# Token transform of a fused attention and Fourier kernel: even and odd tokens apart, on four 32-row parts of the TensorE array

## The chip, the cores and the metric

The kernel runs on one core of a Trainium2 chip. The metric is the device time of one execution in microseconds (us). A core has the engines that the profile calls PE (TensorE, matmuls), DVE (VectorE), ACT (ScalarE), POOL (GpSimd) and SP (SyncE, which here only issues DMAs). Each engine works through its own queue in order; they wait for each other by semaphores.

## The reference, cut to what matters

All in float32. Chunked attention gives `x`; then a Fourier mix over tokens and channels, of which the real part is added; then a normalised two-layer MLP.

```python
q, k, v: (8 batches, 8 heads, 576 tokens, 64)      # chunks of 64 tokens
attn = softmax(q_c @ k_c.T / 8);  x = attn @ v_c    # -> x: (8, 576, 512)
mixed = real(fft(fft(x, axis=tokens), axis=channels))
u = x + mixed
un = (u - mean) / sqrt(var + 1e-6)                  # over channels
out = u + relu(un @ w_ch1) @ w_ch2                  # 512 -> 2048 -> 512
```

The change is about the first of the two transforms: over the 576 tokens, for each of 8 batches. A real input needs cosine and sine sums at frequencies 0 to 288 only; the others follow by mirroring.

## The kernel before, in words

**Tiles.** 128 tokens by 512 channels. A batch of 9 chunks has two LO tiles (chunks 0 to 3), two HI tiles (chunks 8 to 5, held mirrored) and half of a REST tile (chunk 4), which it shares with its neighbour. A *group* is four tiles that go through the MLP together: 8 groups of LO and HI tiles, one per batch, and a last one of the four REST tiles.

**Order.** It is written out by hand. The main loop at the end of the kernel steps through `mlp(g)`, group after group. After each step it lets a *side* generator run on by a share that is counted out so that the side is done when group `g + 1` is due: `side(b)` is `attention(b)`, a pause of three steps, then `fourier(b)`. What a generator does between two `yield`s is put into the engines' queues between two steps of the MLP. In groups 2 to 8 a step is mostly eight matmuls of 128x128 by 128x256. The weights are converted during the first group (`round_weight`), and combined and kept in DRAM (`keep1`, `keep2`) so that the later groups need seven half-size products in place of eight; SP fetches these in slabs (`fetch`).

**From attention to transform.** A token n and its mirror 576 - n share cosine and sine up to sign, so `fold(b, i)` adds and subtracts LO and HI tile and does the same over channels: `pm` has four parts T of 128 channels, and one column more for channel 256. For tokens to stand opposite their mirrors, the first row of each LO chunk has to move on by one chunk: `shift(b)` does this for five rows (L485 to L489), from batch 2 on with six DMAs in SP's queue, through a small tile `first`.

**`fourier(b)`, b from 1 to 7.** For each T it multiplies 128 tokens x 128 channels with the token table `tk` (128 x 289 frequencies), over two full tiles and then the 64 rows of REST: 12 matmuls at L652, and 12 with a single column for channel 256. T = 0, 1 come between one pair of steps, T = 2, 3, REST and the single columns between the next pair. ACT takes the four results out of PSUM into `zf` and `zr` (L678 to L688); then comes the channel transform, three or two times `mixed(i)` (L700), and DVE and POOL add it to x. Batch 0 has its own form, `fourier_early`, before the main loop. In `attention_early`, `turn_tables` (L252 to L254, ACT) reorders the loaded table into `tk`.

**`store(n, o)`** writes a finished tile: one DMA for LO, two for HI, all from SP; four for REST, half of them from ACT in the last group.

Of the kernel before, what the change touches and what calls it, by code (L numbers as in the profile page):

```python
# [8 lines left out]
FP32 = mybir.dt.float32  # L9
# [7 lines left out]
def kernel(  # L17
# [67 lines left out]
    tk = const.tile([128, NM + 1, 2, NQ], FP32, name="tk")  # L85
# [3 lines left out]
    so = const.tile([128, HQ], FP32, name="so")  # L89
    wa = const.tile([128, KD * DFF], FP32, name="wa")  # L90
# [71 lines left out]
    pms, sts = {}, {}  # L162
    start = one_p.tile([128, KF * 512], FP32, tag="big", name="start")
# [5 lines left out]
    v_ring = [const.tile([128, 2, NJ, DV], FP32, name=f"v{i}") for i in range(3)]  # L169
    more_v = one_p.tile([128, 4 * NL + 64], FP32, tag="zf", name="more_v")  # L170
# [4 lines left out]
    def load(n, which="qk"):  # L175
# [4 lines left out]
        for src, dst, nm, eng in ((q, qs, "q", nc.sync), (k, ks, "k", nc.scalar if n == 0 else nc.sync)):  # L180
            if nm not in which:
                continue
            if n < first[1]:
                i = 2 * n + (nm == "k")
                t = start[:, (4 + i) * DM:(5 + i) * DM].rearrange("p (j r d) -> p j (r d)", r=2, d=D)
            else:
                t = one_p.tile([128, NJ, 4 * D], FP32, tag=nm, name=nm)
# [36 lines left out]
    def load_tables():  # L224
# [4 lines left out]
        t = start[:, 0:(NM + 1) * 2 * NQ].rearrange("p (i r f) -> p i r f", i=NM + 1, r=2)  # L229
        for c in range(2 * NM):  # L230
            (i, r0), (j, p0) = divmod(c * CH, 128), divmod((NC - 1 - c) * CH, 128)
            nc.sync.dma_start(out=t[r0:r0 + CH, i], in_=seq_tab[p0:p0 + CH, j])
        for r0 in (0, CH):
            nc.sync.dma_start(out=t[r0:r0 + 1, NM], in_=seq_tab[0:1, 0])
            nc.sync.dma_start(out=t[r0 + 1:r0 + CH, NM], in_=seq_tab[1:CH, NM])
# [11 lines left out]

    def turn_tables():
        t = start[:, 0:(NM + 1) * 2 * NQ]
        a, b = tk.rearrange("p i r f -> p (i r) f"), t.rearrange("p (i f) -> p i f", f=NQ)  # L250
        for c in range(2 * NM):
            nc.scalar.copy(a[:, :, c * CH:(c + 1) * CH], b[:, :, (c + 1) * CH:c * CH:-1])  # L252
        nc.scalar.copy(a[:, :, NL:NL + 1], b[:, :, 0:1])
        nc.scalar.copy(a[:, :, NL + 1:NQ], b[:, :, NL + 1:NQ])  # L254
# [157 lines left out]
    def att_P(n):  # L412
# [3 lines left out]
        nc.scalar.copy(t, pt)  # L416
# [46 lines left out]

    def shift_early(i):

        lows = [xt(at[LO, 0, j])[:, 0:DM] for j in range(NM)]
        rest, kept = xt(rests[0])[0:1, 0:DM], first_rest[0:1, 0:DM]
        if i == 0:
            nc.gpsimd.tensor_copy(kept, lows[1][0:1])
            nc.gpsimd.tensor_copy(lows[1][0:1], lows[1][CH:CH + 1])  # L470
            nc.gpsimd.tensor_copy(lows[1][CH:CH + 1], rest)
        else:
            nc.scalar.copy(rest, lows[0][0:1])
            nc.scalar.copy(lows[0][0:1], lows[0][CH:CH + 1])
            nc.scalar.copy(lows[0][CH:CH + 1], kept)

    def shift(b):

        lows = [xt(at[LO, b, i]) for i in range(NM)]
        r = b % 2 * CH  # L480
        rest = xt(rests[b // 2])[r:r + 1, 0:DM]
        eng = nc.gpsimd if b < 2 else nc.sync
        t = three_p.tile([128, XW], FP32, tag="y", name="first")
        for i in range(NM):
            eng.dma_start(out=t[2 * i:2 * i + 2, 0:DM], in_=lows[i][0:CH + 1:CH, 0:DM])  # L485
        eng.dma_start(out=t[2 * NM:2 * NM + 1, 0:DM], in_=rest)
        for i in range(NM):
            eng.dma_start(out=lows[i][0:CH + 1:CH, 0:DM], in_=t[2 * i + 1:2 * i + 3, 0:DM])
        eng.dma_start(out=rest, in_=t[0:1, 0:DM])  # L489

    def fold(b, i):
# [7 lines left out]
        if i < NM:  # L499
            pm = two_p.tile([128, DM + 1], FP32, tag="pm", name="pm")  # L500
# [5 lines left out]
        else:  # L506
            pm = two_p.tile([128, 2 * HQ + 1], FP32, tag="pm_rest", name="pm_rest")
# [10 lines left out]
        if i < NM:  # L518
# [3 lines left out]
            to = pm[:, 3 * HQ:DM + 1:HQ]  # L522
        else:
            for T, op in enumerate((ALU.add, ALU.subtract, ALU.subtract, ALU.add)):
                to = pm[T % 2 * CH:T % 2 * CH + CH, T // 2 * HQ:T // 2 * HQ + HQ]
                eng.tensor_tensor(out=to, in0=near[:, T // 2], in1=far[:, T // 2], op=op)
            to = pm[CH:, HQ:2 * HQ + 1:HQ]
        eng.tensor_copy(to, two[p, HM + 1 + HQ:HQ - 1:-HM - 1])
        pms[b, i] = pm

    def attention_early():
# [33 lines left out]
        turn_tables()  # L565
# [64 lines left out]
    zr = const.tile([128, 4, 2, CH], FP32, name="zr")  # L630
# [12 lines left out]

    def fourier(b):
        h = b % 2
        zf = one_p.tile([128, 4 * NL + 64], FP32, tag="zf", name="zf")
        zf = zf[:, 0:4 * NL].rearrange("p (t f) -> p t f", t=4)
        pm = [pms.pop((b, i)) for i in range(NM + 1)]

        def product(T, i, out_, lhsT, start, stop, cols=slice(0, NQ)):  # L650
            p = slice(0, 128) if i < NM else slice(T % 2 * CH, T % 2 * CH + CH)
            nc.tensor.matmul(  # L652
                out=out_, lhsT=lhsT[p], rhs=tk[p, i, T // 2 if T != 5 else 0, cols],
                start=start, stop=stop, skip_group_check=True,
            )


        z = [ps_t.tile([128, 512], FP32, tag="pt", name="z") for _ in range(2)]
        more = ps_a.tile([128, 2, 512], FP32, tag="att", name="more_z")
        z += [more[:, k] for k in range(2)]  # L660
        for T in range(4):
            for i in range(NM):
                product(T, i, z[T][:, 0:NQ], pm[i][:, T * HQ:(T + 1) * HQ], i == 0, False)
            if T == 1:
                yield
        for T in range(4):
# [629 lines left out]
```

## Time and profile before

| what | value |
|---|---|
| runs | 1093.8, 1089.85, 1092.42 us; median 1092.42 |
| profiled execution | span 1089.0 us; no time of its own is listed apart from the three runs, of which the lowest is 0.85 us and the median 3.4 us above the span |
| busy share of the span | PE 98%, DVE 53%, ACT 27%, POOL 26% |
| granted TensorE clock | full speed in all 40 slices |
| chain that ended last | PE 89%, DVE 4%, ACT 2%, DMA 2%, SP's queue 2% |
| L652, token transform | PE share of the chain 1.5% (`z`) and 1.7% (`more_z`) |
| end of the last matmul's record | about 1084.2 us, then DVE, the last DMAs, the end |

In the trace one float32 matmul of the code stands as two MATMULs, each with a LDWEIGHTS; counts below are those of the trace unless "of the code" is said. A line of the timeline gives the start, the time from the first start to the last end, the engine, the line of code, what is written and read, the shape and how many. Because matmuls are pipelined, the step from one start to the next, not the duration, is what one costs.

### The profile page before, as it was taken

The page shows a single profiled execution, that of the slowest core. Times are in us where ns is not written, and L with a number is a line of the kernel's source. Part 1 is how long each engine was busy: PE and PEld are TensorE (multiplying, and loading weights), DVE is VectorE, ACT ScalarE, POOL GpSimd, SP SyncE. Part 2 cuts the span into 40 slices and gives each one's busy share as a digit, 9 for nine tenths or more (in the row PEclk, how much of TensorE's full clock was granted, in tenths as well). Part 3 has the DMA queues.
Part 4 walks back from the last instruction along what each step waited for, and adds up shares of the span by engine and source line. Part 5 has one row for each costly group of instructions (what it writes and reads, how often), then busy time and mean ns, then how long its engine had stood idle before and what let it go on. Part 6 is the DMA issues. An engine that isn't in the chain of part 4 may idle for free.

```text
span 1089.0 us, 18837 instructions
## 1 busy us (share of the span) xinstructions
PE 1070.4 (98%) x7018; PEld 848.7 (78%) x7018; DVE 577.2 (53%) x1258; ACT 299.2 (27%) x730; POOL 280.3 (26%) x403
## 2 busy tenths in 40 slices
PE   8999999999999999999999999999999999999998
PEld 6644454446888888888888888888888888888887
DVE  4899987314566355663556455735663534323411
ACT  4788453222113310322022212321133103101300
POOL 4301002444405140153114220514051401210140
PEclk9999999999999999999999999999999999999999
DMA  7777556679575637692668357854653455446232
GB/s 167 224 222 175 158 162 227 171 239 308 178 203 167 198 136 206 189 255 95 191 184 253 124 165 223 206 170 152 197 185 90 147 190 163 120 154 211 78 116 78
DMA packets 147970, 192.73 MB, mean 177 GB/s; under 512 B 66126, under 2 KB 104014, under 8 KB 140712
## 3 DMA queue, kind: packets, MB, share of 16 engines
q1 hardware_dynamic: 145620, 190.20, 58.4%
q8 instruction: 56, 0.92, 0.4%
q0 software_dynamic: 512, 0.68, 0.3%
q10 hardware_dynamic: 1748, 0.66, 0.2%
q14 instruction: 34, 0.28, 0.1%
HBM read 167.22 MB, written 24.12 MB: 176 GB/s over the span
## 4 chain that ended last, share of the span: by engine, by line
PE 89%; DVE 4%; ACT 2%; DMA 2%; SPq 2%; issue 1%; POOL 0%; DVEq 0%; ACTq 0%
PE pb L1089 20%; PE pa L1040 17%; PE pa L1089 15%; PE pb L1040 13%; PE up L973 4%; PE up L953 3%; PE pt L333 3%; PE dn L994 3%; PE mix L700 2%; PE sc L384 2%; PE more_z L652 2%; PE xp L432 2%; PE z L652 1%; PE idle L1167 1%; DMA xall<-in_moe_w_ch_dram 1%; SPq L195 1%
## 5 line engine op out<-in xcount | busy, mean ns | idle before, releaser
L1040 PE MATMUL pa<-unT,wa 128*128 128x256 f32 x672 | 159.5, 380 | 1.1 <-DVE wa L1048 1.1
L1040 PEld LDWEIGHTS pa<-unT,wa 128*128 128x128 f32 x672 | 126.5, 190 | 18.9 <-DVE wa L1048 1.5
L941 POOL TENSOR_TENSOR h<-h 128x256 f32<-128x256 f32 x64 | 55.7, 877 | 269.5 <-PE pb L1040 150.5
L1089 PE MATMUL pa<-wb,h 128*128 128x256 f32 x512 | 115.6, 380 | 0.0
L1089 PE MATMUL pb<-wb,h 128*128 128x256 f32 x512 | 114.9, 379 | 0.0
L1040 PE MATMUL pb<-wa 128*128 128x256 f32 x448 | 106.6, 381 | 0.0
L1089 PEld LDWEIGHTS pa<-wb,h 128*128 128x128 f32 x512 | 96.1, 190 | 13.5 <-issue 0.5
L1089 PEld LDWEIGHTS pb<-wb,h 128*128 128x128 f32 x512 | 96.3, 190 | 12.6
L1040 PEld LDWEIGHTS pb<-wa 128*128 128x128 f32 x448 | 84.2, 190 | 11.6 <-DVE h L1056 0.2
L994 PE MATMUL dn<-wb,h 128*128 128x512 f32 x128 | 58.4, 605 | 0.9 <-ACT h L964 0.9
L1046 DVE TENSOR_TENSOR wa<-pb,wa 128x256 f32<-128x256 f32 x56 | 23.5, 423 | 65.5 <-ACT wa L1045 65.5
L1089 PE MATMUL pb<-wb,yall 128*128 128x256 f32 x256 | 58.2, 381 | 0.0
L1089 PE MATMUL pa<-wb,yall 128*128 128x256 f32 x256 | 57.9, 380 | 0.0
L1089 PE MATMUL pb<-wb 128*128 128x256 f32 x256 | 57.7, 379 | 0.0
L973 PE MATMUL up<-unT,wa 128*128 128x512 f32 x128 | 56.8, 596 | 0.0
L1045 ACT COPY wa<-pa 128x256 f32<-128x256 f32 x56 | 20.8, 372 | 125.1 <-PE pa L1040 125.1
L1040 PE MATMUL pa<-wa 128*128 128x256 f32 x224 | 53.5, 382 | 0.0
L717 POOL TENSOR_TENSOR xall<-y,xall 128x513 f32<-128x513 f32 x14 | 21.3, 1518 | 125.3 <-DVE y L711 125.3
L1040 PE MATMUL pb<-unT,wa 128*128 128x256 f32 x224 | 52.9, 379 | 0.0
L1089 PEld LDWEIGHTS pa<-wb,yall 128*128 128x128 f32 x256 | 47.7, 190 | 6.4
L1089 PEld LDWEIGHTS pb<-wb,yall 128*128 128x128 f32 x256 | 47.7, 190 | 6.3
L1089 PEld LDWEIGHTS pb<-wb 128*128 128x128 f32 x256 | 47.6, 190 | 5.9
(250 smaller groups left out, 1685.0 us busy)
## 6 DMA issues: line engine op xcount, KB each, us to landing
wb<-s SPq DMA_DIRECT2D x56, 1024.0 KB
wa<-s SPq DMA_DIRECT2D x196, 256.0 KB
xall<-in_moe_w_ch_dram SPq DMA_DIRECT2D x22, 512.0 KB
q<-in_q_dram SPq DMA_DIRECT2D x96, 112.0 KB
k<-in_k_dram SPq DMA_DIRECT2D x96, 112.0 KB
v<-in_v_dram SPq DMA_DIRECT2D x124, 64.0 KB
yall<-in_moe_w_ch_dram SPq DMA_DIRECT2D x10, 512.0 KB
s<-wb SPq DMA_DIRECT2D x20, 256.0 KB
```

Source lines behind the costliest of these rows:

```text
L333: nc.tensor.transpose(pt[:, j, :], src(j), ident)
L384: nc.tensor.matmul(out=sc[t0:t0 + CH, e, j * CH:(j + 1) * CH], lhsT=a[r0:r0 + D, 2 * j + c, 0:CH], rhs=b[r0:r0 + D, 2 * j + c, 0:CH], star ...
L432: nc.tensor.matmul(out=xp[0][e][t0:t0 + CH, j * DV:(j + 1) * DV], lhsT=a[r0:r0 + CH, j, t0:t0 + CH], rhs=b[r0:r0 + CH, c, j, :], start=Tru ...
L652: nc.tensor.matmul(out=out_, lhsT=lhsT[p], rhs=tk[p, i, T // 2 if T != 5 else 0, cols], start=start, stop=stop, skip_group_check=True,)
L700: nc.tensor.matmul(out=mix[:, cols], lhsT=zt[:, T], rhs=tab, start=(T == 0), stop=(T == 3), skip_group_check=True,)
L941: nc.gpsimd.tensor_tensor(out=h1[:, m, hi], in0=h1[:, m, lo], in1=h1[:, m, hi], op=ALU.subtract)
L953: nc.tensor.matmul(out=up, lhsT=w1[:, kk, m * 128:(m + 1) * 128], rhs=unT[:, kk], start=(kk == 0), stop=(kk == KD - 1), skip_group_check=True,
L973: nc.tensor.matmul(out=up, lhsT=w1[:, kk, m * 128:(m + 1) * 128], rhs=unT[:, kk], start=(kk == 0), stop=(kk == KD - 1),)
L994: nc.tensor.matmul(out=dn, lhsT=h1[:, m, s * 128:(s + 1) * 128], rhs=w2[:, m, :], start=(m == 0), stop=(m == KF - 1),)
L1040: nc.tensor.matmul(out=dst, lhsT=w[:, kk, r], rhs=rhs[o][:, kk], start=(o in (0, 1) and kk == 0), stop=(kk == 1), skip_group_check=True,)
L1046: nc.vector.tensor_tensor(out=b, in0=pbs[r][:, 0], in1=a, op=ALU.add)
L1089: nc.tensor.matmul(out=dst, lhsT=lhs[:, m], rhs=w[:, m], start=(o in (0, 2) and m == 0), stop=(m == HF - 1), skip_group_check=True,)
```

## The change

It rewrites the token transform of batches 1 to 7, and reorders the tokens of each chunk for it.

- Tokens of a 64-token chunk are held with 32 of one parity first, then 32 of the other. `att_P` does this while it copies the transposed probabilities out of PSUM (same ACT copy, other access pattern). `store` and the table loads follow the order.
- The table `tk` shrinks to frequencies 0 to 144 (NE = 145). For frequency f and 288 - f the sums over even tokens are equal up to sign, and so are those over odd tokens; so even and odd sums are formed apart, and then E + O and E - O give both halves.
- `z_sets` computes these with matmuls of 32 rows: four of the code in a row, one for each 32-row part, each to another PSUM bank. 40 such matmuls of 32x128 by 32x145 per batch, in two sets ("turns") of 24 and 16, take the place of 12 of 128 or 64 rows by 289.
- `mid_products`: the single column for channel 256, now two columns (as it is, and with the sign of the parity, made by one more small operation in `fold`); 12 matmuls of one column as before.
- ACT copies the odd sums (`z_odd`), DVE forms sum and difference (`z_joined`), ACT then spreads the result into `zf` and `zr` (`z_tile`, `z_rest`). There is one more `yield`, and `sizes` counts one more.
- The table is loaded once, in full length, to a part of `wb`; `fourier_early` uses it from there, and ACT copies the half that is kept to `tk` after step 8. `turn_tables` is gone.
- `shift` for b > 1 is six GpSimd copies of one row each, in place of six DMAs of SP.
- `store`: two DMAs for LO, four for HI of which ACT issues two, five for REST.
- Three unused tiles are allocated as padding, and some tiles are declared elsewhere.

```diff
-    tk = const.tile([128, NM + 1, 2, NQ], FP32, name="tk")
+    NE = NQ // 2 + 1
+    tk = const.tile([128, NM + 1, 2, NE], FP32, name="tk")
...
+    const.tile([128, 48], FP32, name="pad_a")
...
-        nc.scalar.copy(t, pt)
+        nc.scalar.copy(
+            t.rearrange("p j (c r i) -> p (j c) r i", c=2, r=2), pt.rearrange("p j (c i r) -> p (j c) r i", c=2, r=2)[:, :, ::-1]
+        )
...
-        eng = nc.gpsimd if b < 2 else nc.sync
+        eng = nc.gpsimd
         t = three_p.tile([128, XW], FP32, tag="y", name="first")
+        if b > 1:
+            kept, r0, r1 = t[0:1, 0:DM], slice(ODD, ODD + 1), slice(ODD + CH, ODD + CH + 1)
+            a, c = lows[0][:, 0:DM], lows[1][:, 0:DM]
+            for to, from_ in ((kept, rest), (rest, a[r0]), (a[r0], a[r1]), (a[r1], c[r0]), (c[r0], c[r1]), (c[r1], kept)):
+                eng.tensor_copy(to, from_)
+            return
...
         eng.tensor_copy(to, two[p, HM + 1 + HQ:HQ - 1:-HM - 1])
+        eng.tensor_tensor(out=pm[rows, m0 + 1:m0 + 2], in0=pm[rows, m0:m0 + 1], in1=sign[rows], op=ALU.mult)
...
-        turn_tables()
...
+    def z_sets(z, pm, i, turn_, first=False):
+        for s in range(2):
+            for q_ in range(4):
+                k, r = (q_ // 2 + turn_) % 2, q_ % 2
+                T, p = 2 * k + s, slice(32 * q_, 32 * q_ + 32)
+                d0_ = T * HQ if i < NM else s * HQ
+                nc.tensor.matmul(
+                    out=z[r][k][:, s * NE:(s + 1) * NE], lhsT=pm[i][p, d0_:d0_ + HQ],
+                    rhs=tk[p, NM - 1 - i if i < NM else NM, k],
+                    start=first and s == 0, stop=False, skip_group_check=True,
+                )
...
+    def z_odd():
+        for k in range(2):
+            nc.scalar.copy(zs[0][:, 2 * k:2 * k + 2, 1], zs[2][k][:, 0:2 * NE].rearrange("p (t f) -> p t f", t=2))
+
+    def z_joined():
+        even = zs[1][:, :, 0:2 * NE].rearrange("p k (t f) -> p k t f", t=2)
+        z4 = zs[0].rearrange("p (k t) r f -> p k t r f", t=2)
+        nc.vector.tensor_tensor(out=z4[:, :, :, 0], in0=even, in1=z4[:, :, :, 1], op=ALU.add)
+        for k in range(2):
+            e, o = even[:, k], z4[:, k, :, 1]
+            a, b = (e, o) if k == 0 else (o, e)
+            nc.vector.tensor_tensor(out=o, in0=a, in1=b, op=ALU.subtract)
...
+        z = z_space()
         for i in range(NM + 1):
+            z_sets(z, pm, i, 0, i == 0)
+        outs = [z[0][0][32 * g:32 * g + 1, 2 * NE:] for g in range(4)]
+        for i in range(NM):
+            mid_products(outs, pm, i)
+        nc.scalar.copy(middle[:, 0, 0:1], outs[0][:, 0:1])
+        yield b == 1
+        if b == 1:
+            yield
+        mid_products(outs, pm, NM)
+        for i in range(NM):
+            z_sets(z, pm, i, 1)
+        z_middle(outs)
+        z_odd()
+        if b == 1:
+            z_joined()
+        else:
+            yield
+            z_joined()
+        nc.scalar.copy(zs[0][0:1, 2], middle)
+        if h == 1:
+            z_rest(h)
+        for i in range(NM):
+            z_tile(zf, i)
+        if h == 0:
+            z_rest(h)
+        yield b == 1
...
+            elif kind(n) == RE:
+                eng = nc.scalar if last and h else nc.sync
...
             else:
-                nc.sync.dma_start(out=out[b, t0:t0 + CH, :], in_=o[r0:r0 + CH])
+                for r in range(2):
+                    eng = nc.scalar if r else nc.sync
+                    eng.dma_start(out=out[b, t0 + 1 - r:t0 + CH:2, :], in_=o[r0 + ODD * r:r0 + ODD * r + ODD])
+        if kind(n) == RE:
+            eng.dma_start(out=out[b - 1:b + 1, 0, :], in_=o[LONE])
...
+                if t == 8:
+                    nc.scalar.copy(tk, early_tk[:, :, :, 0:NE])
```

`z_tile` makes five ACT copies of at most 256 elements per partition, `z_rest` five smaller ones, `z_middle` four of one row.

## The prediction

> **What bounds the kernel now.** I read the busy table first, then the chain that ended last, then the timeline of PE around one `fourier(b)`.
>
> ```profile
> PE 1070.4 (98%) x7018; PEld 848.7 (78%) x7018; DVE 577.2 (53%) x1258; ACT 299.2 (27%) x730; POOL 280.3 (26%) x403
> ...
> PE 89%; DVE 4%; ACT 2%; DMA 2%; SPq 2%; issue 1%; POOL 0%; DVEq 0%; ACTq 0%
> ```
>
> PE is busy throughout and is 89% of the chain, the others have half their time free. So what leaves PE's queue is nearly a gain of the same size, and what is added elsewhere costs only if PE must wait for it. The block of batch 7 (the last column before a bracket is the count):
>
> ```profile
> 827.90 2.11 PE L652 MATMUL z<-tk,pm 128*128 128x289 f32 x8
> 829.85 1.89 PE L1040 MATMUL pa<-unT,wa 128*128 128x256 f32 x8
> 831.58 2.11 PE L652 MATMUL more_z<-tk,pm 128*128 128x289 f32 x8
> 833.62 0.76 PE L652 MATMUL z<-tk,pm_rest 64*128 64x289 f32 x4
> 834.21 0.66 PE L652 MATMUL more_z<-tk,pm_rest 64*128 64x289 f32 x4
> 834.79 0.43 PE L652 MATMUL more_z<-tk,pm 128*1 128x73 f32 x16
> 835.16 0.30 PE L652 MATMUL more_z<-tk,pm_rest 64*1 64x73 f32 x8
> 835.39 0.48 PE L1089 MATMUL pa<-wb,h 128*128 128x256 f32 x1
> ```
>
> From start to start: 8 full MATMULs of 289 columns take 829.85 - 827.90 = 1.95, or 0.244 each. Four with 64 rows take 0.59, where one after the other would be 0.98: two run at a time. Sixteen with one output column take 0.37; at 0.244 x 73 / 289 = 0.062 each that would be 0.99: they run four at a time. The rest of each stretch, 0.10 to 0.12, is the change from one form to the next. The first MATMUL after it has 0.48 in place of 0.38: its weights were not loaded ahead (0.10). The block costs 1.95 + (835.39 - 831.58) + 0.10 = **5.86**, seven blocks 41.
>
> **What the Trainium skill says.** "TensorEngine Tiling (Array Packing)", Key Properties: parts of the array load weights and multiply in parallel, and a change of the tiling mode drains the engine. The trace agrees: two or four at a time, 0.10 to 0.12 for a change. Same page, Restrictions and Gotchas: row parts that run together must write to different PSUM banks. In the changed code the bank is z[q_%2][(q_//2+turn)%2], four banks for four parts; before, `z` and `more_z` did so for two parts. "TensorE: Matmul & The Clock Gate", Part 3: four parts of 32 rows gave 3.07x, not 4x (512 columns). No run here shows four row parts; the nearest row is `sc`, four quarters of 64x64 at a time:
>
> ```profile
> 283.18 0.69 PE L384 MATMUL sc<-kT,qT 64*64 64x64 f32 x32
> 283.80 0.91 PE L1089 MATMUL pb<-wb,h 128*128 128x256 f32 x3
> ```
>
> 32 in 0.62; 8 slots of 64 columns are 8 x 0.054 = 0.43, and 0.19 is getting in and out. So four at a time cost little more than one.
>
> **The change, part by part.**
>
> *Token products.* 40 matmuls of the code, 80 MATMULs of 145 columns. One needs 0.244 x 145 / 289 = 0.122; loading 128 weight columns needs no more than 0.113 (two 128x128 `mix` products start 0.225 apart). I take 0.125 a slot: 80 / 4 x 0.125 = 2.50. The single columns stay 24 MATMULs, 6 slots of 0.062 = 0.37. Changes of form: in, to columns, out, in both halves, 6 x 0.12 = 0.72, and a weight load not hidden (0.10) at two entries and two exits, 0.40. Sum 3.99, gain 5.86 - 3.99 = 1.87, **seven times -13.1**. With the skill's 3.07 in place of 4 the slots are 3.26 and the gain is 7.8.
>
> *Evacuation.* ACT has 18 operations a block as before, of about the same sizes, and DVE three new ones, about 0.7 + 0.42 + 0.42 = 1.5 (estimate from L710, 255 elements in 0.42). The chain from the last token product to `mix` is longer: `z_odd`, DVE 1.5, the copy of the middle row 0.4, `z_rest` about 1.0 (odd b). From batch 2 on two MLP steps (2 x 3.45) stand between the join and `mix`, and the join of odd batches first waits for two DVE adds (0.84) at the end of the up half: 3.7 of 6.9. Cost nothing; if that cover is gone, what exceeds 6.9, per block. One more wait: the last single columns wait for a one-element ACT copy issued a step earlier; hidden likewise. The even banks are held a stage longer, but no `turn` or score matmul falls into that stage.
>
> *Batch 1* has one step as cover, and today it stalls:
>
> ```profile
> 152.06 0.49 PE L700 MATMUL mix<-ce,zr 128*128 128x129 f32 x2 [1.12 <-ACT zr L681]
> 152.51 0.49 PE L700 MATMUL mix<-co,zr 128*128 128x128 f32 x2
> 153.82 1.22 PE L700 MATMUL mix<-cx,zr 128*128 128x256 f32 x2 [0.82 <-ACT zr L688]
> 154.83 0.63 PE L700 MATMUL mix<-so,zr 128*128 128x128 f32 x2
> ```
>
> These four took 3.2 to the next `dn`, against 1.1 in batch 7, after 1.1 of waiting: 3.2 lost, because ACT stood behind weight conversion. In the change two of the three gaps put no conversion ahead, but the chain is 0.8 + 0.8 + 1.5 + 0.4 + 1.0 = 4.5 against a step of 3.4. So 1 to 2 are lost in place of 3.2. I take **-1.0** (from -2.2 to +1.5).
>
> *`shift`.* In SP's queue its six DMAs of batch 4 stand from 455.38 to 459.6, ahead of weight slabs and the next q and k. The chain shows what that led to:
>
> ```profile
> 456.05 1.78 DMA first<-xall
> ...
> 462.14 4.16 DMA q<-in_q_dram
> ...
> 467.84 1.99 PE pa L1040 x8
> ```
>
> PE lost 1.2 ahead of 467.84; the other batches' DMAs delayed nothing that shows. Gone: **-1.2** (0 to -1.5). On POOL six copies at 0.60 (L469, 1x512) are 3.6 a batch, six batches. Behind them wait `fold` and the subtraction L941, which the down half needs only in its fourth product, over 20 us later; POOL is 74% idle. Nothing. The sign column adds three operations of 0.2 per `fold`: POOL for b > 1, DVE for b = 1, hidden by the pause of three steps.
>
> *Start.* Without `turn_tables` the first token product need not wait for ACT until 31.77; the warm-up matmuls end at 31.45: -0.3. `zr` takes 15 ACT operations in place of 10, at a spacing of 0.09, before L641, which had 0.21 of slack: +0.25. SP issues ten table DMAs in place of eight, so the channel tables come up to 0.6 later; POOL is done with them at 37.6 and PE wants them at about 38.9: covered. The copy of `tk`, 870 elements by the rate of L252 (384 in 0.44) 1.0, is among ACT's ReLUs, between 0 and +1.0; I take **+0.3** for the whole start.
>
> *`store`.* SP: six `shift` DMAs less, two LO stores more per batch. ACT now issues two DMAs for each of 16 HI tiles behind a DVE result, and, as built, behind an earlier DMA of SP's queue. Behind them in ACT's queue is `pT`, which PE needs a step (3.45) later: 0.42 + 0.65 + 0.58 = 1.65, so 1.8 of slack, which a late SP can use up. Not shown in the trace; between 0 and +4, I take **+1.0**. At the end ACT issues three DMAs in place of two: **+0.3** (L883, 0.26 to 0.36).
>
> *Padding* moves addresses only; nothing in the trace prices it. PE's MATMULs already start 0.216 apart for 256 columns, so 0, from -1 to +1.
>
> Sum: -13.1 - 1.0 - 1.2 + 0.3 + 1.0 + 0.3 = **-13.7** on the span of 1089.0: 1075.3. The median of the runs is 3.4 above that span; I keep this: 1078.7.
>
> **Rivals.**
>
> *A. Four row parts run at 3.07.* For it: the skill's figure. Against: `sc` at four a time. 5.3 less gain: 1084.
>
> *B. Only two at a time, slower.* The two passes of a matmul sit on the same part, so a queue kept strictly in order would overlap neighbours only. Against: the 0.59 for four REST MATMULs includes the first weight load, so passes are interleaved, and `sc`. Place: L676; price: 40 slots, +2.5 a block, 17.5 in all: 1096. The gain of all parts is gone below 2.2 at a time (slots of 4.46 per block).
>
> *C. ACT's queue becomes the wait.* HI stores hold ACT for SP, `pT` or `unT` comes late, PE idles 0.5 to 1 at each of 16 tiles: 1086 to 1094. For: two queues now in series. Against: SP has fewer DMAs.
>
> *D. `mix` waits in every block,* 1 to 2 each, if DVE is behind: 1086 to 1093. Against: DVE 53% busy, about 3 of slack.
>
> *E. The queue was not the cause:* q and k come late in batch 4 all the same: +1.2, inside the range.
>
> **How the numbers follow.** Forecast as summed 0.58, A 0.20, C 0.08, B 0.08, D 0.06. About 0.3% (3.3 us) is what a measurement of this kernel can tell from no change. Faster than 1089: the forecast, A, and part of C and D, 0.83. Same: rest of C and D, 0.06. Slower: B, and C or D at their worst or together, 0.11. Range: below, all unknowns at their good end, about 1071; above, past A to where C begins, 1089.
>
> **What would show it.** Right: the 24 and 16 row-part matmuls take 1.7 and 1.2 (0.125 a slot), L676 and L686 together about 4.0 a block; no `first` DMA in SP; no idle of PE before `mix` beyond 1 from batch 2 on. Wrong: 0.16 a slot or more (A), 0.25 (B), PE released by ACT `pT` next to a store (C), `mix` released by ACT `zf` or `zr` (D).

## The result: 3.65% slower

After the change the kernel takes 1129.07 us (median of 4 runs, 1127.49 to 1136.71) against 1091.96 before in the same comparison: ratio 1.0365, 95% interval 1.0338 to 1.0392. The profiled execution took 1130.52 us, its span is 1128.7. The prediction was 1078.7 and "faster": wrong, by 50 us. The token products, which bring the gain, behaved as predicted; five things around them, each costed at next to nothing or not at all, and some smaller ones lost more than three times what was gained.

The page of the kernel after, busy table and chain that ended last:

```profile
PE 1069.4 (95%) x7410; PEld 847.0 (75%) x7410; DVE 586.3 (52%) x1287; ACT 308.6 (27%) x730; POOL 306.6 (27%) x459
...
PE 74%; DMA 4%; issue 2%; SPq 1%; DVE 1%; POOL 1%; ACT 1%; DVEq 0%; POOLq 0%; ACTq 0%
```

PE's busy time is the same as before (1070.4), although it has less to do, and its share fell from 98% to 95%. The chain of the kernel after reaches back only to 162 us, so its shares sum to 84% and the 74% cannot be set against the 89% of before; of the 951.7 us that it covers PE has 87%. The loss is better counted so: between its first and its last MATMUL PE is idle for 42.6, where it was 12.5; it is busy 1.0 less; and 10.6 more pass behind its last MATMUL. That makes the 39.7 by which the spans differ. PE is busy no less because the clock that it was granted is half over 44.4 us of this trace ahead of the last MATMUL (3.4 before). PE is busy in 28.5 of these, so about 14 us of its busy time (an estimate, half of 28.5) are due to the slow clock. The question, then, is who ends each stop of PE.

First the gain. The block of batch 7, timeline of PE (start, duration, line, operation, last the count; the lines shown stand for slots of four MATMULs that run side by side):

```profile
855.43 0.39 PE L676 MATMUL z<-tk,pm 32*128 32x145 f32 x1
...
855.66 0.28 PE L676 MATMUL z<-tk,pm 32*128 32x145 f32 x1
...
855.78 0.28 PE L676 MATMUL z<-tk,pm 32*128 32x145 f32 x1
...
857.12 0.43 PE L686 MATMUL z<-tk,pm 128*1 128x73 f32 x16
857.48 0.92 PE L1149 MATMUL pa<-unT,wa 128*128 128x256 f32 x3
...
861.13 0.30 PE L686 MATMUL z<-tk,pm_rest 64*1 64x73 f32 x8
...
862.57 1.13 PE L1149 MATMUL pa<-unT,wa 128*128 128x256 f32 x4
```

In the whole list four MATMULs start within 0.02, and the next four 0.12 later: four at a time, 0.122 a slot. The block costs (857.48 - 855.43) + (862.57 - 861.13) = 3.49, with two late weight loads (0.20) 3.69, where it was 5.86. The gain, 2.2 a block, is there in the trace, and a little more than predicted (1.87).

Where the loss came in. A group has an up half (products with `w_ch1`) and a down half (products with `w_ch2`). From the first MATMUL of each half in the two traces (after minus before, in us): start +1.9; up half of group 0 +10.4, its down half +0.7; up half of group 1 +15.0, down half -4.1; group 2 -1.6; group 3 +7.7 and -4.2; group 4 -1.0; group 5 +10.4 and -4.2; group 6 -1.9; then flat; behind the slot of the last MATMUL +10.6 (5.0 became 15.6). Sum 39.7, the difference of the spans. (In groups 1, 3 and 5 about 2.2 only moved from the down half to the up half, with the first token products; net of that the gain is 2.0 a block, the losses are 12.8, 5.5 and 8.2.)

The stops behind these numbers, timeline of PE after; the bracket holds the idle time ahead and what ended it. In the text a stop is given as what it costs, about 0.17 more than the bracket: a MATMUL of 256 columns has a record of 0.38 but a slot of 0.216.

```profile
126.74 6.58 PE L1103 MATMUL dn<-wb,h 128*128 128x512 f32 x8 [6.03 <-ACT h L1073]
...
234.91 1.14 PE L396 MATMUL sc<-kT,qT 64*64 64x64 f32 x32 [10.21 <-DVE rd L459]
...
713.85 3.78 PE L1149 MATMUL pa<-unT,wa 128*128 128x256 f32 x8 [3.76 <-DVE wa L1157]
```

The third line shows a second price of such stops: eight products that take 1.89 elsewhere took 3.78. The granted clock (`PEclk`, the third number behind the stretch) was half there:

```profile
40.40:43.81 3.41, 3.41 (x9) 0.50 1.08 335
712.82:719.65 6.83, 5.80 (x14) 0.50 0.89 246
```

The Trainium skill, "TensorE: Matmul & The Clock Gate", Part 1, names such a state (half clock after about 3.4 us of idling, full clock again after as much work). This trace agrees for the stop of 3.76. But shorter idling was enough as well: 2.84 in run 14 below, and here, at 40.40, two idles of 0.58 and 0.81 close together; in the kernel before, at 153.63, two of 1.12 and 0.82 (3.41 us at half clock, which the profile's 40 slices of 27 us do not show). The measurement decides.

Three views say what was waited for. First DVE's timeline ahead of the first stop, after and then before the change:

```profile
105.44 0.69 DVE L470 TENSOR_TENSOR xall<-xp,rd 128x512 f32<-128x512 f32 x1
115.40 0.43 DVE L320 TENSOR_SCALAR wb<-xall 128x512 uint32<-128x512 uint32 x1 [9.27 <-DMA xall<-first]
```

```profile
103.54 0.69 DVE L456 TENSOR_TENSOR xall<-xp,rd 128x512 f32<-128x512 f32 x1
104.15 0.42 DVE L308 TENSOR_SCALAR wb<-xall 128x512 uint32<-128x512 uint32 x1
```

Then SP's queue and DVE ahead of the second stop:

```profile
220.30 1.10 SPq L984 DMA_DIRECT2D out_dram<-o  x2
221.51 2.03 SPq L992 DMA_DIRECT2D out_dram<-o  x2
223.71 3.82 SPq L203 DMA_DIRECT2D k<-in_k_dram  x4
```

```profile
233.78 1.08 DVE L364 STREAM_TRANSPOSE kT<-k 128x512 f32<-128x512 f32 x1 [13.48 <-DMA k<-in_k_dram]
234.72 0.16 DVE L459 TENSOR_SCALAR rd<-xp 128x4 f32<-128x4 f32 x2
```

And the chain ahead of the stop of group 3, at 478.70:

```profile
465.85 5.23 DMA q<-in_q_dram
...
471.10 6.02 DMA k<-in_k_dram
...
478.24 0.42 DVE wa L1157
...
478.70 3.78 PE pa L1149 x8
```

First stop: a weight conversion (L320) stands 9.27 us for the DMAs of `shift(1)`; before the change the conversions did not wait for these. Second: PE waits for DVE's `rd`, which stands behind the reordering of k (L364), and this waits 13.48 for the load of k. By the semaphores SP, on its way through the four loads, stood until 226.2 for an LO store (L984) that it had issued at 217.8; the last load went out at 227.1 and landed 6.5 later. Third: DVE's `wa` stands behind the reordering of k in the same way; q and k take 5 to 6 us to land, and SP issues this k only when q has landed. The chain that ended last does not pass through the second stop: ahead of 250 it leads through GpSimd, where `keep1` is idle for 15.94. My first guess, the copies of `shift` in GpSimd's queue, was read from there and was wrong (run 3).

### The profile page after: what moved, and what is told of

Same layout as the page of the kernel before. It is cut to its first block, busy times and chain, and to the rows that moved or that the text cites. A ratio compares the mean times of both kernels' runs of the same rounds, so it can differ in the third digit from the quotient of the medians.

```text
span 1128.7 us, 19754 instructions
## 1 busy us (share of the span) xinstructions
PE 1069.4 (95%) x7410; PEld 847.0 (75%) x7410; DVE 586.3 (52%) x1287; ACT 308.6 (27%) x730; POOL 306.6 (27%) x459
## 4 chain that ended last, share of the span: by engine, by line
PE 74%; DMA 4%; issue 2%; SPq 1%; DVE 1%; POOL 1%; ACT 1%; DVEq 0%; POOLq 0%; ACTq 0%
PE pb L1198 20%; PE pa L1149 16%; PE pa L1198 15%; PE pb L1149 12%; PE up L1082 3%; PE pt L345 2%; PE mix L795 1%; DMA q<-in_q_dram 1%; PE z L676 1%; PE dn L1103 1%; DMA k<-in_k_dram 1%; PE xp L446 1%; DMA v<-in_v_dram 1%; SPq L203 1%; PE sc L396 1%
## 5 line engine op out<-in xcount | busy, mean ns | idle before, releaser
L1149 PE MATMUL pa<-unT,wa 128*128 128x256 f32 x672 | 164.2, 388 | 8.9 <-DVE wa L1157 8.9
L1103 PE MATMUL dn<-wb,h 128*128 128x512 f32 x128 | 61.7, 633 | 6.0 <-ACT h L1073 6.0
L1163 ACT ACTIVATE h<-pa 128x256 f32<-128x256 f32 x56 | 21.5, 383 | 120.7 <-PE pa L1149 115.3
L1168 DVE TENSOR_TENSOR h<-pb,wa 128x256 f32<-128x256 f32 x56 | 23.7, 424 | 51.8 <-PE pb L1149 51.8
```

Source lines behind the costliest of these rows:

```text
L1103: nc.tensor.matmul(out=dn, lhsT=h1[:, m, s * 128:(s + 1) * 128], rhs=w2[:, m, :], start=(m == 0), stop=(m == KF - 1),)
L1149: nc.tensor.matmul(out=dst, lhsT=w[:, kk, r], rhs=rhs[o][:, kk], start=(o in (0, 1) and kk == 0), stop=(kk == 1), skip_group_check=True,)
L1163: nc.scalar.activation(out=h1[:, m, lo], in_=dst, func=ACTF.Relu)
L1168: nc.vector.tensor_tensor(out=h1[:, HF + m, lo], in0=dst, in1=b, op=ALU.add)
```

## The experiments

18 kernels, each compared with the kernel before on the same chip. Where nothing else is said, a run is the changed kernel with the edit shown. "Gain" is the difference of ratios times 1091 us, against the changed kernel (1.0365) unless another run is named; by the intervals a gain is uncertain by 3 to 4 us where single edits are compared, and by about 1 in run 7. Runs 5, 7, 8, 10 and 12 leave the tokens of each LO chunk in mirrored order in the output: they tell what the order of the store costs, and are not versions to use.

**1. The tail.** The REST store writes 32 and 31 rows; the 31 are split.

```
-  eng.dma_start(out=out[b, t0 + 2:t0 + CH:2, :], in_=o[r0 + ODD + 1:r0 + CH])
+  eng.dma_start(out=out[b, t0 + 2:t0 + CH // 2 + 1:2, :], in_=o[r0 + ODD + 1:r0 + ODD + 17])
+  eng.dma_start(out=out[b, t0 + CH // 2 + 2:t0 + CH:2, :], in_=o[r0 + ODD + 17:r0 + CH])
```

> The changed kernel with each 31-row output DMA of a REST tile split into 16 and 15 rows; nothing else differs. In the changed kernel the last DMA landed 15.6 us after the last MATMUL, before the change 5.0. Theory (the 31 rows go one after another on one DMA engine, about 0.08 us a row, 2.5 us a DMA, and the DMAs of the last four tiles stand behind one another): the tail comes down to 5 to 7, the time by 8 to 10, to about 1.028 of the kernel before. Rival (the tail is the issue of more DMAs by ACT and SP and their waits for older DMAs): two more DMAs per tile, so the tail stays at 15 or grows by 1 to 2, time 1.036 to 1.038.

Measured: 1.028 (1.0256 to 1.0304), gain 9.3. The last issues, timelines of after and then of this run:

```profile
1113.42 0.42 DVE L1218 TENSOR_TENSOR wb<-pb,wb 128x256 f32<-128x256 f32 x1 [3.10 <-PE pb L1198]
1116.88 0.34 ACTq L987 DMA_DIRECT2D out_dram<-wb  x1
...
1119.67 0.54 ACTq L994 DMA_DIRECT2D out_dram<-wb  x1
```

```profile
1112.53 0.42 ACTq L988 DMA_DIRECT2D out_dram<-wb  x1
...
1113.55 0.54 ACTq L995 DMA_DIRECT2D out_dram<-wb  x1
1113.94 0.32 SPq L988 DMA_DIRECT2D out_dram<-wb  x1
1114.30 0.61 SPq L989 DMA_DIRECT2D out_dram<-wb  x1
```

The kernel before issued its last one at 1085.10, 3.9 ahead of its end:

```profile
1085.10 0.36 ACTq L883 DMA_DIRECT2D out_dram<-wb  x1
```

In the kernel after, the final result stands at 1113.84, but its store is issued at 1116.88, since issuing waited for older stores, and the span ends 1128.7. In the trace's packets the 31 rows of a DMA go one behind another, 0.08 us a row, and where two such DMAs overlap their rows take turns at that spacing: they share one DMA engine. The Trainium skill, "DMA: Bandwidth & Descriptors", under why a DMA increments its semaphore by 16, gives the rule: the number of DMA engines is the largest up to 16 that divides the slowest dimension of both sides. 31 is prime, so one; by the same rule 16 and 15 rows get 16 and 15, and the 63 rows of the kernel before got 9. The records of the semaphores agree: a store of 31 rows updates its semaphore 2 times, one of 63 rows 10 times, one of 16 or of 15 rows 16 times. With the split the last issue is at 1114.30 and the span ends 2.7 later: the theory held, with its size.

**2. `shift(1)`.** Copies by GpSimd, as for the later batches.

```
-        if b > 1:
+        if b > 0:
             kept, r0, r1 = ...
```

> The changed kernel with shift(1) done by six GpSimd copies, as for the later batches, in place of six DMAs of GpSimd's queue. In the changed kernel DVE stood 9.3 us at 115.40 ahead of a weight conversion (L320), the down half of group 0 began at 126.7, 12.2 later than before the change. Theory (the conversion waits for the DMAs that write xall): the wait is gone, the down half begins at 116 to 119, and the time falls by 8 to 10, to about 1.028 of the kernel before. Rival (DVE was behind for what it had to convert, or waits for the rows however they are moved): 0 to -3; six copies of 0.6 on GpSimd come in place of DMAs and fold(1, 1) comes later by up to 3.6.

Measured: 1.029 (1.0267 to 1.0313), gain 8.2; the down half of group 0 begins at 120.6 in place of 126.7, a little past the expected 119. DVE's timeline:

```profile
107.41 0.69 DVE L470 TENSOR_TENSOR xall<-xp,rd 128x512 f32<-128x512 f32 x1
108.01 0.42 DVE L320 TENSOR_SCALAR wb<-xall 128x512 uint32<-128x512 uint32 x1
108.34 0.83 DVE L323 TENSOR_SCALAR power<-xall 128x512 uint32<-128x512 uint32 x1
109.10 1.09 DVE L333 SCALAR_TENSOR_TENSOR wb<-xall,wb 128x512 f32<-128x512 uint32 x1
```

The wait is gone; a stop of 2.7 ahead of the down half is left. That the DMAs cause the wait is shown; why the program has the conversion wait for rows 32 and 96 where it did not wait for rows 0 and 64 stays open.

**3. `shift(b)`, b > 1, back to SP's queue.** `eng = nc.gpsimd if b < 2 else nc.sync`, and the six DMAs.

> The changed kernel with shift(b) for b > 1 back in SP's queue as six DMAs, on the new rows 32 and 96. Theory (the six copies stand in GpSimd's queue until attention is through, behind them keep1's operations, in SP's queue behind these the q and k loads that attention needs): PE's stop of 10.4 us at 234.9 is gone, time -11 to -13, to about 1.025. If the copies are the cause of the stops of 3.8 at 478.7 and 713.9 too, another -10 and 1.015. Rival (the stop at 234.9 comes from the two-stage join and its yields): the stop stays, 1.036 to 1.039, since SP has the DMAs back.

Measured: 1.0517 (1.0495 to 1.0539), slower by 16.6. The stop at 234.6 is still 10.4, so the copies do not cause it: the theory fell. New stops of 4.2 and 2.7 appear in batches 3 and 5. Moving `shift` off SP is a gain in the changed kernel. The chain of this run, ahead of the same stop, gave the next lead:

```profile
220.01 0.94 SPq L984
...
221.00 10.58 DMA out_dram<-o
231.65 0.65 SPq L226
```

SP stood until an LO store (L984) had landed, 10.58 us after its issue.

**4. Both HI stores from SP.** `eng = nc.sync` in place of `eng = nc.scalar if r else nc.sync`.

> The changed kernel with both halves of each HI store issued by SP; ACT issues no store but the last REST ones. Theory (ACT stands behind its own output DMAs, 56 us of waits in sum ahead of the copy L1154, and these hold PE in batches 4 and 6): those waits go, the stops of PE at 478.7 and 713.9 shrink, time -5 to -13, 1.025 to 1.032. Rival (these waits of ACT are covered; the stops come from late q and k, which SP's queue sets): 0, or up to +4 since SP has 16 more DMAs ahead of its loads, 1.036 to 1.040.

Measured: 1.0384 (1.0356 to 1.0412), no difference that this run can tell from 1.0365, and the stops stay. That ACT issues half of the HI stores is not the cause.

**5. LO rows stored in rising order.** The LO store of a chunk, 64 rows, writes tokens backwards and every second one, so in DRAM its slowest dimension is 2. In the kernel before, one store of 128 rows wrote the same bytes in all, and its slowest dimension was 2 as well. In this run the rows go out in rising order, 32 at a time; the tokens of each LO chunk then stand mirrored in the output.

```
-  to = out[b, t0 + 1:t0 + CH + 1, :][::-1].rearrange("(i r) d -> r i d", r=2)[::-1]
-  nc.sync.dma_start(out=to, in_=o[r0:r0 + CH])
+  for r in range(2):
+      nc.sync.dma_start(out=out[b, t0 + 1 + r:t0 + CH + 1:2, :], in_=o[r0 + ODD * r:r0 + ODD * r + ODD])
```

> The changed kernel, but the LO store writes the rows of each chunk in rising order of tokens, one DMA of 32 rows per parity, so the tokens of a chunk stand mirrored in the output; nothing else differs. In the changed kernel (and before) this store's slowest dimension in DRAM is 2, and its last byte lands 8 to 14 us after its issue, where a DMA of 32 rows with one dimension lands after 2 to 3. Theory (the store runs on two DMA engines; q and k loads issued behind it on SP's queue wait for it there, 9 us in place of 3, and its semaphore stays taken): PE's stops at 234.9 (10.4), 478.7 (3.8) and 713.9 (3.9) go, with the slow clock behind them: time -18 to -26, ratio 1.013 to 1.020. Rival (SP's queue is late by its own waits and the number of DMAs, or by GpSimd's keep1): stops stay, 1.034 to 1.038.

Measured: 1.0235 (1.0204 to 1.0265), gain 14. The stops shrink, from 10.4 to 4.4, from 3.8 to 2.4 and from 3.9 to 1.9, but do not go. The first of them (timeline of PE):

```profile
227.84 0.69 PE L396 MATMUL sc<-kT,qT 64*64 64x64 f32 x32 [4.27 <-DVE rd L459]
```

By the rule above the store runs on two DMA engines, and its semaphore is updated 3 times, where that of a store of 32 rows is updated 16 times. In the kernel after its last update comes 6 to 11 us after the issue (the expectation's 8 to 14 was too long), in this run mostly after 1.6 to 3. That the slow store costs time is shown, its share was put too high. Two ways lie open and this run does not part them: SP stands until the store has landed, as ahead of the second stop and in run 3, and loads that are issued behind it share its two engines.

**6. LO stores by ACT, HI stores by SP.**

> The changed kernel with the LO stores issued by ACT and both halves of the HI stores by SP: the same DMAs in the right order, but the slow store stands in ACT's ring and no longer in SP's ahead of the q and k loads. Theory (q and k queue behind the store in the same ring): part of the gain of the run with rising rows, -8 to -20, ratio 1.018 to 1.029. Rival (the two DMA engines themselves are the limit whichever ring, or ACT stands behind its stores): 0 to -5, or worse by up to 5: 1.032 to 1.041.

Measured: 1.0467 (1.0443 to 1.0491), slower by 11; the stop of batch 2 is 12.1. The theory fell. The rival was right, and past its end of the range; which of its two reasons held this run does not tell.

**7. The kernel before with LO rows in rising order**, one DMA of 128 rows.

> The kernel before the change, with its LO store written in rising order as one DMA of 128 rows, so the tokens of a chunk stand mirrored in the output. Theory (the store on two DMA engines was there before, 12 to 14 us long, but fell where no load was due, save once, the stop of 1.2 us at 467.84, and 1.6 at 227.83): -1 to -3, ratio 0.997 to 0.999. Rival (the store costs the kernel before nothing): 1.000.

Measured: 0.9958 (0.9946 to 0.997), gain 4.6, more than either expected: the stops at 227.83 and 467.84, 2.8 together, are gone. The store now lands after 2.0 to 5.5, where it took 7.8 to 12.3. The second stop before, and the same products in this run (timelines of PE):

```profile
467.84 1.99 PE L1040 MATMUL pa<-unT,wa 128*128 128x256 f32 x8 [1.05 <-DVE wa L1048]
```

```profile
465.20 1.89 PE L1040 MATMUL pa<-unT,wa 128*128 128x256 f32 x8
```

So the two-engine store had a price in the kernel before as well. This run still has the six DMAs of `shift` in SP's queue: they alone did not cause the stop at 467.84, to which the prediction had put it down.

**8. Rising rows, split REST stores and `shift(1)` by copies together** (edits 5, 1, 2).

> The changed kernel with three edits together: LO rows stored in rising order (tokens of a chunk mirrored in the output), the 31-row REST stores split into 16 and 15, and shift(1) by GpSimd copies. If the three causes are separate, their gains add: -9 (tail), -8.5 (shift) and -18 to -26 (stores) from 1129, that is 1086 to 1094; if they cover one another, more is left. The prediction's 1078.7 would be met only if nothing else was lost: what stays above it is the part that no edit of these explains (start +1.9, batch 1).

Measured: 1.0055 (1.0038 to 1.0072), 1096.31 us. The three gains sum to 31.7, together they give 33.8: they are separate. But stops of 4.9 in batch 2, 3.4 in batch 4 and 2.3 in batch 6 are left, so something else holds q and k.

**9. No pauses for the planner in batch 1.** A side generator that yields True makes the main loop skip weight conversion in that step. In the change `fourier(1)` does so twice; here it no longer does.

```
-        yield b == 1
+        yield
```

> The changed kernel with `yield` in place of `yield b == 1` at the two places in fourier(b), so that in these steps of batch 1 the planner goes on with weight conversion, as before the change. In the changed kernel keep2 began at 183.6 on DVE, in the kernel before at 153.7; its DMAs are then issued all together from 185 on and SP is late into group 1. Theory (the conversions put off in batch 1 set SP late, so q and k late in batch 2): keep2 begins 8 to 20 us earlier, the stop of PE at 234.9 falls from 10.4 to under 5, time -5 to -9, ratio 1.029 to 1.032. Rival (SP is late from its own stores alone, and the conversions now stand ahead of the join in batch 1): the stop stays, mix waits 1 to 3 more, ratio 1.036 to 1.040.

Measured: 1.032 (1.0294 to 1.0347), gain 4.9. `keep2` begins at 170.7 in place of 183.6 on DVE (153.7 before the change), the stop of batch 2 falls from 10.4 to 4.9, but `mix` of batch 1 now waits 6.5. The theory held, at its last point of the range (1.032); the rival was right that batch 1 waits longer, and wrong that the stop stays. The pauses buy time in batch 1 and pay more in batch 2, by a difference that is barely clear of the noise here; run 17 repeats it.

**10. The same with edits 5, 1, 2.**

> The run with rising LO rows, split REST stores and shift(1) by copies (tokens of an LO chunk mirrored in the output), and `yield` in place of `yield b == 1`. That run stood at 1.0055 with a stop of 4.9 at 218.2 and one of 1.0 at 233.5 in batch 2. Theory: both go, time -5 to -8, ratio 0.998 to 1.001. Rival: batch 1 loses what batch 2 gains, 1.004 to 1.007.

Measured: 1.0027 (1.0013 to 1.004), gain 3.1 against run 8, under the 5 to 8 expected: a stop of 2.9 is left in batch 2, and batch 1 waits 6.7.

**11. A version with all rows in place: LO stores by GpSimd** (`nc.gpsimd.dma_start(out=to, ...)`), edits 1, 2, 9.

> A version with all rows where they belong: the changed kernel with split REST stores, shift(1) by copies, `yield` in place of `yield b == 1`, and the LO stores issued by GpSimd in place of SP. Theory (q and k wait behind the LO store in SP's ring on the two DMA engines that it uses, and SP's issue is relieved of four DMAs a group): near the run with rising rows, ratio 0.997 to 1.006. Rival (the two engines are the limit whoever issues, or GpSimd's own DMAs hold its queue, with fold and the copies of shift behind them): 1.010 to 1.025.

Measured: 1.0024 (1.0011 to 1.0037), as good as run 10. The store still takes 7.5 us to land (median), but in GpSimd's queue it does no more harm than a fast one in SP's. So a slow store does not hold the kernel whoever issues it, which was the first of the rival's reasons in run 6.

**12. Run 10 without the step before the join.** The change put one more `yield` between the second half of the token products and `z_joined`, and counts one more step in `sizes`.

```
         else:
-            yield
             z_joined()
...
-   ... + PAUSE + 3 + NM + b % 2)
+   ... + PAUSE + (3 if b == 1 else 2) + NM + b % 2)
```

> As the run with rising rows, three edits and plain yields (tokens of an LO chunk mirrored in the output), and also without the step between the second half of the token products and the join for b > 1, sizes smaller by one. With the step PE stops 3.4 at 460.6 and 2.3 at 690.7, batches 4 and 6. Theory (the longer side sequence shifts the q and k loads against the slab fetches): these stops go, time -4 to -7 against that run. Rival (they come from the slab fetches and stores in SP's queue, or mix now waits for the join): 0 or slower by up to 4.

Measured: 0.9965 (0.9949 to 0.998), gain 6.8. The stops of batches 4 and 6 are gone, as the theory had it, and that of batch 2; instead `mix` of the even batches waits 1.3 to 1.7 for the join, the wait that the step was covering.

**13. The changed kernel without this step, nothing else.**

> The changed kernel without the step between the second half of the token products and the join for b > 1 (sizes smaller by one there); nothing else differs, the LO stores stay in SP's queue. Theory (the step moves the q and k loads ahead against stores and slabs; without it they fall between them as before the change): the stops of batches 4 and 6 go, that of batch 2 shrinks, time -8 to -20, ratio 1.018 to 1.029. Rival (the slow LO stores hold q and k whatever the step): 0 to -5, 1.032 to 1.037.

Measured: 1.0266 (1.0249 to 1.0282), gain 10.8. The stops of batches 4 and 6 fall from 3.8 and 3.9 to 2.1 and 1.4; that of batch 2 stays at 10.8, against what I expected.

**14. The kernel before with such a step**, empty, after the evacuation, `sizes` one more.

> The kernel before the change with one more empty step in fourier(b) after the evacuation of the token products, sizes larger by one, as the change has it. Theory (the step alone moves the loads into the stores and slabs): PE stops of 2 to 4 in batches 2, 4 or 6, time +3 to +12, ratio 1.003 to 1.011. Rival (the step does no harm without the change's stores and copies): 0.999 to 1.001.

Measured: 1.0175 (1.0162 to 1.0188), slower by 19, well past the expected range. Timeline of PE and chain of this run:

```profile
343.50 3.51 PE L1041 MATMUL pa<-unT,wa 128*128 128x256 f32 x8 [3.12 <-DVE wa L1049]
...
463.08 3.23 PE L1041 MATMUL pa<-unT,wa 128*128 128x256 f32 x7 [2.84 <-DVE wa L1049]
```

```profile
437.92 9.75 DMA out_dram<-wb
...
448.09 7.31 DMA q<-in_q_dram
...
456.27 5.23 DMA k<-in_k_dram
```

The step is empty, yet PE stops 2 to 5 us in each of batches 2 to 6. As I read it, one more step in the count moves every attention step a little against the MLP's steps, and with it the q and k loads in SP's queue against the LO store and the 1 MB slabs; I followed this for batch 4 only. There the load of q waits 9.75 for the store and then takes 7.31. (The place is not quite that of the change, where the step stands before the join and for b > 1; batch 1 has its additional step elsewhere.)

**15 and 16. Without the step, edits 1 and 2, pauses kept: LO stores by GpSimd, and by SP.**

> A version with all rows where they belong: the changed kernel with split REST stores, shift(1) by copies, LO stores issued by GpSimd, and without the step before the join; the planner's pauses of batch 1 are kept. Theory (the gains add): batch 1 waits 1 to 3 in place of 7, batch 2 stops 0 to 4, ratio 0.990 to 0.998. Rival (GpSimd's DMAs or the put-off conversions give it back): 0.998 to 1.006.

> As the version with LO stores by GpSimd and without the step, but the LO stores stay in SP's queue. Theory A (without the step the slow stores fall where no load is due, as in the kernel before): same as that version within 2 us. Theory B (they hold q and k of batch 2 in SP's ring all the same): slower than it by 5 to 12, ratio 1.000 to 1.008, the stop in batch 2 at 5 to 10.

Measured: 1.0022 (1.001 to 1.0034) and 1.0092 (1.0079 to 1.0106). The store in SP's queue costs 7.6 even without the step (theory B). The first is not faster than before, as the rival had it: batch 2 stops 9.7 at 219, which the next runs put down to the pauses.

**17 and 18. The version of run 15 with plain `yield`, and with one of the two pauses.**

> All rows where they belong: split REST stores, shift(1) by copies, LO stores by GpSimd, no step before the join, and plain `yield` in fourier(1), so that no conversion is put off. Theory (put-off conversions make SP late into batch 2): the stop of 9.7 at 219 falls to 0 to 3, mix of batch 1 waits 7 in place of 1, PE's other stops of batch 1 (2.2, 0.8) go: time -3 to -7 against the version with both pauses, ratio 0.995 to 0.999. Rival: the stop stays, and batch 1's wait comes on top: 1.003 to 1.008.

> As the version with plain yields, but the pause of the planner is kept in the step of the first half of batch 1's token products, and dropped in the step of the join. Theory (each put-off conversion is worth about the same): between the two others, mix waits 3 to 5 and the stop of batch 2 is 3 to 6, ratio 0.996 to 1.001. Rival (the conversions that hurt mix are those of one step alone): mix 1 to 2 and the stop under 4, 0.991 to 0.996.

Measured: 0.9966 (0.9955 to 0.9977), 1087.64 us, and 0.9974 (0.9965 to 0.9984). With no pause there is no stop in batch 2; batch 1 pays once (timeline of PE, run 17):

```profile
159.80 0.80 PE L794 MATMUL mix<-ce,zr 128*128 128x129 f32 x2 [6.40 <-ACT zr L742]
```

With one pause `mix` waits 1.2 twice, PE stops 3.2 at 175.9, and 1.8 and 1.2 in batch 2: the stop is between that with none and that with both. The time lies in the theory's range and is no better than with none.

Run 17 has all rows in place and beats both kernels: by 0.34% the one before, by 3.85% the changed one (0.9966 / 1.0365). Its busy table:

```profile
PE 1057.9 (97%) x7410; PEld 841.0 (77%) x7410; DVE 593.4 (55%) x1287; ACT 310.0 (29%) x730; POOL 328.5 (30%) x491
```

## Why the prediction was wrong, point by point

The gains measured one by one (9.3 tail, 8.2 `shift(1)`, 14.2 LO store, 4.9 pauses, 10.8 step) sum to 47.4; the run with all five (12) stood 43.6 below the changed kernel. Forecast and result lie 53.5 apart (39.8 lost, 13.7 promised), so these five explain about four fifths, give or take the noise of each; the rest is at the end of this section. What failed in the prediction is thus not its main term but the terms of the sum that it put at nothing or nearly so:

- **Token products, right.** Predicted 0.125 a slot, 1.7 and 1.2 for the row-part MATMULs of the two halves, 3.99 a block; measured 0.122, 1.69 and 1.20, and 3.69: 2.2 gained a block where 1.9 was forecast. Rivals A and B are out.
- **Evacuation at nothing: the failed step that weighs most in method.** The prediction named the cover of `mix`, two MLP steps, and did not price what made it two: the added `yield` and the larger `sizes`. The cover itself is worth 1.3 to 1.7 in three batches; the step costs 10.8 in the changed kernel, and 19, empty, in the kernel before. What it moves is named in run 14, the q and k loads against the store and the slabs; why they then take so long was not followed further. Rival D (`mix` waits) did not come about in the changed kernel, because of that step.
- **Batch 1, -1.0: the failed step was to count what the pauses put first and not what they put back.** "Two of the three gaps put no conversion ahead" was right as far as it went: `mix` waited 1.2 where 3.2 were lost before (of these 3.2 a part was the half clock from 153.63 on). But the conversions came later, so `keep2` began 30 us later than before, 13 of them by the pauses (run 9), SP issued its DMAs in a lump, and q and k of batch 2 were late: 4.9. (The prediction's own figures, 1 to 2 lost in place of 3.2, would have given -1.2 to -2.2 and not -1.0.) A stop of 2.2 ahead of `turned(1, 0)`, at 183.7, belongs to this too: it is in no run with plain `yield`.
- **`shift`, -1.2: right in sign, but for a reason that fell, and incomplete.** The stop of 1.2 went in run 7 with these DMAs left in place, so rival E, late q and k whatever `shift` does, was right in the main; in the kernel after that stop is 3.8. With the DMAs in SP's queue the changed kernel is 16.6 slower (run 3), so the sign was luck in part. The copies on GpSimd held nothing, as said. What failed is that `shift(1)` was taken as unchanged: its DMAs touch other rows, and a conversion on DVE waited 9.3 us for them, worth 8.2.
- **Start, +0.3: too small.** Measured +1.9. The table DMAs delayed not the channel tables, which I watched, but the weights behind them in SP's queue: a conversion on DVE waits 1.85 for `yall<-in_moe_w_ch_dram`, and PE then waits 0.75 and 0.98 for copies of the first transform, of which DVE does half. That these follow from the late conversion is read from the order on DVE, not tried. The half clock from 40.40 on is not needed for it: run 17 has full clock there and starts 1.6 late.
- **`store`, +1.0 for ACT and nothing for SP.** ACT's part was right or below what run 4 can tell, so rival C falls. SP's part failed: "two LO stores more per batch" are two more DMAs on two DMA engines, each landing only after 6 to 11 us, with SP and the loads of q and k behind it: 14.2 in the changed kernel. The kernel before paid 4.6 for its own.
- **Tail, +0.3: the term was sized by the issue of a DMA and not by its landing.** Measured +10.6, of which 9.3 are the 31 rows.
- **Padding at nothing:** not tried by itself.

What stays open: run 17 ends 3.7 below the kernel before, not 13.7. By the starts of its halves it gains 10.9 from group 1 on, six blocks at 1.8, since `mix` waits in the even ones; ahead of that it loses 6.9 (start 1.6, up half of group 0 2.7, its down half with the wait of `mix` in batch 1 2.6), and 0.7 behind the last MATMUL. The 2.7 in group 0 goes with a stop of 2.7 ahead of the first `dn` in all versions with copied `shift(1)`. In run 2 DVE's conversions took 0.83 and 1.09 beside the copies, in place of 0.42 and 0.69, about 1.2 in all; whether the rest is order was not tried.

## What to carry to other kernels

Price a DMA by how many DMA engines its slowest dimension gives it and by its landing, not by its issue: here stores of 31 rows and stores with a leading dimension of 2 cost 23.5 together, more than the 15.4 that the matmuls saved, through whatever waited behind them. Where the order of several engines is counted out by hand, a step or a pause added to the count is an edit with its own price: try it alone, empty, in the kernel before. And for every operation that is put off, follow what it feeds, to the loads at the end of that chain.

## What the runs showed of the hardware that I had not expected

- Four parts of 32 rows gave a full four in this kernel: 0.122 a slot of 145 columns, where 3.07 in place of 4 would have been 0.16.
- A stop of PE of some 3 us costs nearly double: the eight products after it took 3.78 (idle 3.76) or 3.51 (idle 3.12) in place of 1.89. Two short idles can do the same: after 0.58 and 0.81 the 14 products from 39.62 on took 5.04, where run 17 needs 3.44. In these traces the half clock comes, up to the last MATMUL, in stretches of 3.41 or two, three or four times that.
- The updates of a store's semaphore bear out the rule quoted in run 1: 2 for 31 rows, 3 for a leading dimension of 2, 10 for 63 rows, 16 for 15 rows, each one more than the engines of the rule, and 16 for 16 or 32 rows.
- DVE operations on SBUF ran at 1.09 in place of 0.69 while GpSimd copied single rows of 512 elements (run 2, 109.10 beside copies from 108.23 to 110.66), so a copy moved to GpSimd was not free for DVE there.
